# The v loads of all 24 tiles moved from SyncE's DMA queue to ScalarE's, with a priority for each kind of load and six buffers for a and v

## The chip, the cores and the metric

One core of one Trainium2 chip. The metric is the device time of one execution in microseconds, as the median of the runs of a kernel. Times are compared between kernels that ran in turn on the same chip.

## The reference, cut to what matters

```python
# B, H, S, D = 4, 8, 768, 40
def _attn_ref(r, k, v, w, a, b):
    state = zeros((B, H, D, D))
    for t in range(S):                                   # kt = k[:, :, t] and so on
        y[:, :, t] = einsum('bhd,bhde->bhe', rt, state)
        Sa = einsum('bhde,bhe->bhd', state, at)
        state = (state * wt[:, :, None, :] - einsum('bhd,bhe->bhde', Sa, bt)
                 + einsum('bhd,bhe->bhde', vt, kt))
    return y

def _moe_ref(x, w_theta, w_tok_r, w_tok_i, w_ch):        # x: y as [4, 768, 320]
    theta = x @ w_theta
    y = einsum('ts,bsd->btd', w_tok_r, x * cos(theta)) + einsum('ts,bsd->btd', w_tok_i, x * sin(theta))
    u = x + y
    return u + maximum(u @ w_ch, 0.0)
```

The kernel cuts each sequence of 768 steps into 6 chunks of 128. That makes 24 tiles of 128 steps by 8 heads by 40 features. Each tile needs one load of w, k, b, a and v, of 160 KB each, and half of a pair of r loads.

## The kernel before, the parts that matter

All work is a list of operations. A list scheduler in Python, run when the kernel is built, orders them from tuned priorities and a model of their costs; each engine then runs its operations strictly in that order.

```python
    raw_w = sb("raw_w", [128, H, D], FP32, 4)
    raw_a = sb("raw_a", [128, H, D], FP32, 4)
    raw_kb = sb("raw_kb", [128, 2, H, D], FP32, 4)
    raw_v = sb("raw_v", [128, H, D], FP32, 4)
    # ... load(i) gives for tile i the buffers i % 4 and the sources
    #     ap[bi, :, ci * C:(ci + 1) * C, :].rearrange("h t d -> t h d"), so pieces of 40 floats

    def evac(eng, kind, i, psk, dst, n, reads=(), writes=()):
        if eng == "ACT":
            add(eng, kind, i, lambda: copy_words(dst, ps(psk)[:, 0:n // 2]), 165 + n / 2.4, [psk], writes)
        # ... else the same on DVE

    def loads(i):
        for key, dst, src in load(i):                     # w, k, b, a, v
            add("SP", "load", i,
                lambda dst=dst, src=src: nc.sync.dma_start(out=dst, in_=src),
                650, [], [key], work=1030)
        # ... and two r loads for each pair of tiles, also on SyncE

    # ... prep, attention_scores, recurrence, readout, theta, mixing: all add() operations
    order = plan.order()
    table = "lnexp"
    for o in order:
        # ... a table load where ScalarE's function changes
        o.fn()
```

ScalarE (ACT) works between TensorE (PE) and its next inputs nearly everywhere. It copies transposed blocks and products out of PSUM, the memory that TensorE writes to (`evac`, `nx` and `nu`), and it makes the exponentials `ex`.

## Time and profile before

| | before |
|---|---|
| time, median of 3 runs | 215.06 us (214.36 to 215.53) |
| span in the profile | 212.6 us |
| TensorE busy | 195.1 us, 92% |
| ScalarE busy | 148.6 us, 70% |
| mean granted clock of TensorE | 1.00 |

The lines behind this stand in the prediction below.

### The profile page before, as it was taken

To read this page: it belongs to the slowest core of one execution; us is meant where nothing else is said; L and a number is where in the kernel's file an instruction comes from. 1 tells how busy PE (TensorE), PEld (TensorE's weight loads), DVE (VectorE), ACT (ScalarE), POOL (GpSimd) and SP (SyncE) were. 2 spreads that over 40 slices of the span, in tenths; PEclk is the share of its full clock that TensorE was granted. 3 is DMA by queue.
4 is the path that set the end of the run, shared out by engine and by line. 5 is a ranking of instruction groups with operands and counts; after the bars stand their busy time and mean duration, and the time that the engine had idled before them with its cause. 6 is when DMAs were issued, how large, how long until landed. Compare 5 with 4: busy or idle time off the path is not lost.

```text
span 212.6 us, 8107 instructions
## 1 busy us (share of the span) xinstructions
PE 195.1 (92%) x3344; PEld 156.3 (74%) x3344; DVE 165.5 (78%) x252; ACT 148.6 (70%) x340; POOL 117.4 (55%) x173
## 2 busy tenths in 40 slices
PE   1686899888998999999999999999999999999993
PEld 1464777776786777888878888887788887777771
DVE  7537796989889779869897889978979899744533
ACT  3375858799989969968787676599967996642101
POOL 5003358578765997857688315477667488050000
PEclk9999999999999999999999999999999999999999
DMA  7998989999799999975999899977997110011222
GB/s 118 221 191 170 178 166 175 177 181 185 148 162 194 162 166 193 190 123 111 244 161 197 163 180 178 183 133 172 183 201 145 35 34 3 0 34 71 84 96 93
DMA packets 134181, 30.82 MB, mean 145 GB/s; under 512 B 125824, under 2 KB 134144, under 8 KB 134144
## 3 DMA queue, kind: packets, MB, share of 16 engines
q1 hardware_dynamic: 131712, 27.54, 66.1%
q0 software_dynamic: 2432, 2.77, 8.8%
q8 instruction: 26, 0.43, 0.9%
q14 instruction: 11, 0.09, 0.1%
HBM read 29.13 MB, written 3.93 MB: 156 GB/s over the span
## 4 chain that ended last, share of the span: by engine, by line
PE 78%; DVE 7%; ACT 4%; issue 4%; DMA 3%; POOL 2%; SPq 1%; DVEq 0%; ACTq 0%; POOLq 0%
PE ps_s L724 19%; PE ps_s L398 13%; PE ps_d L522 11%; PE ps_s L670 9%; PE ps_s L625 4%; PE ps_s L573 3%; PE ps_s L505 3%; PE ps_s L591 2%; DVE phi L527 2%; PE ps_s L654 2%; DVE psi L527 2%; PE ps_s L772 2%; DMA raw_v<-in_v_dram 2%; PE ps_d L448 2%; PE ps_s L652 2%
## 5 line engine op out<-in xcount | busy, mean ns | idle before, releaser
L468 POOL TENSOR_TENSOR kb<-raw_kb,ex 128x320 bf16<-128x320 f32 x44 | 37.3, 863 | 32.4 <-ACT ex L460 30.9
L724 PE MATMUL ps_s<-zr,wtok_r 128*128 128x320 bf16 x144 | 40.7, 300 | 0.0
L724 PE MATMUL ps_s<-zi,wtok_i 128*128 128x320 bf16 x144 | 40.6, 299 | 0.0
L527 DVE TENSOR_TENSOR psi<-ps_d,mask_p 128x1024 bf16<-128x1024 f32 x24 | 29.3, 1220 | 7.4 <-PE ps_d L522 7.3
L527 DVE TENSOR_TENSOR lamu<-ps_d,mask_p 128x1024 bf16<-128x1024 f32 x24 | 29.3, 1220 | 4.7 <-PE ps_d L522 4.2
L527 DVE TENSOR_TENSOR lamv<-ps_d,mask_p 128x1024 bf16<-128x1024 f32 x24 | 29.1, 1218 | 3.0 <-PE ps_d L522 2.9
L527 DVE TENSOR_TENSOR phi<-ps_d,mask_n 128x1024 bf16<-128x1024 f32 x24 | 29.2, 1217 | 0.7 <-PE ps_d L522 0.6
L472 POOL TENSOR_TENSOR ah<-raw_a,ex 128x320 bf16<-128x320 f32 x22 | 19.0, 863 | 16.3 <-ACT ex L460 7.6
L706 POOL TENSOR_TENSOR zr<-cs,x 128x320 bf16<-128x320 f32 x23 | 17.8, 791 | 12.9 <-ACT cs L694 12.9
L460 ACT ACTIVATE ex<-ps_d 128x648 f32<-128x648 f32 x24 | 17.2, 716 | 7.7 <-PE ps_d L456 4.6
L734 DVE TENSOR_TENSOR u<-ps_s,x 128x320 bf16<-128x320 f32 x24 | 11.7, 489 | 11.2 <-PE ps_s L724 11.1
L401 ACT COPY uT<-ps_s 128x192 f32<-128x192 f32 x24 | 7.7, 320 | 17.1 <-PE ps_s L625 17.0
L706 POOL TENSOR_TENSOR zi<-cs,x 128x320 bf16<-128x320 f32 x23 | 17.7, 791 | 2.1 <-ACT cs L694 2.0
L522 PE MATMUL ps_d<-aT,kbT 64*128 64x128 bf16 x384 | 17.2, 222 | 1.1 <-ACT aT L401 0.5
L401 ACT COPY kbT<-ps_s 128x512 f32<-128x512 f32 x24 | 14.3, 595 | 4.6 <-PE ps_s L398 3.9
L724 PEld LDWEIGHTS <-wtok_r 128*128 128x128 bf16 x144 | 14.0, 97 | 4.5
L724 PEld LDWEIGHTS <-wtok_i 128*128 128x128 bf16 x144 | 14.0, 98 | 3.6
L398 PE MATMUL ps_s<-ident,kb 128*128 128x128 bf16 x192 | 15.4, 223 | 1.3 <-DVE kb L468 1.3
L743 DVE SCALAR_TENSOR_TENSOR oo<-ps_s,u 128x320 f32<-128x320 f32 x24 | 11.6, 486 | 5.2 <-PE ps_s L670 5.2
L522 PEld LDWEIGHTS <-kbT 64*128 64x128 bf16 x384 | 11.6, 96 | 5.2 <-issue 1.7
L654 PE MATMUL ps_s<-kb,lamu 128*128 128x40 bf16 x192 | 15.0, 180 | 0.5 <-DVE lamu L527 0.4
L652 PE MATMUL ps_s<-kb,lamv 128*128 128x40 bf16 x192 | 15.4, 180 | 0.0
(113 smaller groups left out, 556.3 us busy)
## 6 DMA issues: line engine op xcount, KB each, us to landing
raw_w<-in_w_dram SPq DMA_DIRECT2D x24, 160.0 KB, 3.8
raw_kb<-in_k_dram SPq DMA_DIRECT2D x24, 160.0 KB, 4.3
raw_kb<-in_b_dram SPq DMA_DIRECT2D x24, 160.0 KB, 4.2
raw_a<-in_a_dram SPq DMA_DIRECT2D x24, 160.0 KB, 4.1
raw_v<-in_v_dram SPq DMA_DIRECT2D x24, 160.0 KB, 3.9
raw_r<-in_r_dram SPq DMA_DIRECT2D x24, 160.0 KB, 3.5
out_dram<-oo SPq DMA_DIRECT2D x24, 160.0 KB, 2.3
wrow_r<-in_moe_w_tok_r_dram POOLq DMA_DIRECT2D x6, 192.0 KB, 4.7
```

The costliest lines, as they stand in the source:

```text
L398: nc.tensor.transpose(out=dst[:, c:c + 128], in_=pair(src, g), identity=ident)
L401: nc.scalar.copy(out=out.bitcast(FP32), in_=in_)
L460: add("ACT", "exp", i, lambda: nc.scalar.activation(out=ex, in_=ps(pk).rearrange("p a b -> p (a b)")[:, 512 - DM:512 + DM + 8], func=AF.Ex ...
L468: lambda j=j: (nc.vector if fast else nc.gpsimd).tensor_tensor(out=paired(kb[:, j])[:, :, :, 0:D], in0=natural(raw_kb[s4][:, j]), in1=invW ...
L472: lambda: (nc.vector if fast else nc.gpsimd).tensor_tensor(out=paired(ah)[:, :, :, 0:D], in0=natural(raw_a[s4]), in1=Wi, op=ALU.mult),
L522: nc.tensor.matmul(t[:, q, g, :], lhsT=lhs[rows(q), g * 128:(g + 1) * 128], rhs=rhs[rows(q), g * 128:(g + 1) * 128], start=True, stop=True)
L527: add("DVE", kindm, i, lambda: nc.vector.tensor_tensor(out=dst.rearrange("p a b c -> p (a b) c"), in0=ps(p).rearrange("p a (g c) -> p (a g ...
L652: nc.tensor.matmul(o, lhsT=lamv[:, p, g, :], rhs=kb[:, 0, h, 0:D], start=first, stop=False, skip_group_check=True)
L654: nc.tensor.matmul(o, lhsT=lamu[:, p, g, :], rhs=kb[:, 1, h, 0:D], start=False, stop=True, skip_group_check=True)
L670: nc.tensor.matmul(dst, lhsT=lhs[:, kt, :], rhs=rhs[:, kt, :], start=kt == 0, stop=kt == 2)
L706: nc.vector if fast else nc.gpsimd).tensor_tensor(
L724: nc.tensor.matmul(ps(pk)[:, 0:DM], lhsT=wtok[nm][:, s, j * 128:(j + 1) * 128], rhs=zs[c][:, s], start=n == 0 and c == 0, stop=n == NT - 1 ...
```

## The change

The intent: SyncE's queue is one line, in which a v load stands behind everything else. A second issuing engine lets v come when its own priority says, and deeper buffers for a and v allow earlier loads.

```diff
+SECOND = dict(v=24)
-SP_DEPTH = 3600.0
+SP_DEPTH = 4600.0
@@ priorities: now also one correction per operation, and a term for PE changing its mode
-            o.prio = 1000.0 * (TIMES[o.spec[0]][o.spec[1]] + OFF[o.spec[2]])
+            o.prio = 1000.0 * (TIMES[o.spec[0]][o.spec[1]] + OFF[o.spec[2]] + ADJ.get(o.idx, 0.0))
@@ buffers
-    raw_a = sb("raw_a", [128, H, D], FP32, 4)
+    raw_a = sb("raw_a", [128, H, D], FP32, 6)
-    raw_v = sb("raw_v", [128, H, D], FP32, 4)
+    raw_v = sb("raw_v", [128, H, D], FP32, 6)
@@ loads
+        last = None
         for key, dst, src in load(i):
-            add("SP", "load", i,
-                lambda dst=dst, src=src: nc.sync.dma_start(out=dst, in_=src),
-                650, [], [key], work=1030)
+            name = key[0][4:]
+            if i < SECOND.get(name, 0):
+                add("ACT", "l" + name, i,
+                    lambda dst=dst, src=src: nc.scalar.dma_start(out=dst, in_=src),
+                    430, [], [key], work=930, after=[last])
+            else:
+                last = add("SP", "l" + name, i,
+                    lambda dst=dst, src=src: nc.sync.dma_start(out=dst, in_=src),
+                    600, [], [key], work=930)
@@ cut: all numbers of OFF, TIMES, WAIT, TSWITCH tuned anew; ADJ, a table of 1,456 numbers
```

The scheduler's model charges ScalarE 430 ns for an issue.

## The prediction

> **What bounds the kernel now.** I read first the page's busy times, then the table of stretches (busy time of every engine, clock and DMA share by window), then the chain of work that ended last, the waits of the SyncE queue, and last the queue's timeline.
>
> ```profile
> span 212.6 us, 8107 instructions
> PE 195.1 (92%) x3344; PEld 156.3 (74%) x3344; DVE 165.5 (78%) x252; ACT 148.6 (70%) x340; POOL 117.4 (55%) x173
> ```
>
> TensorE is busiest, but 92% is an average over two very different halves. The table of stretches shows it (columns: window, its length, then busy us and instructions of PE, PEld, DVE, ACT, POOL, then clock, DMA share, GB/s):
>
> ```profile
> 0.00:20.00 20.00, 11.51 (x157) 8.84 (x157) 11.93 (x56) 10.60 (x22) 4.04 (x15) 1.00 0.97 174
> 20.00:70.00 50.00, 44.95 (x907) 36.26 (x908) 42.75 (x46) 41.56 (x98) 33.40 (x49) 1.00 0.97 175
> 70.00:100.00 30.00, 29.50 (x532) 24.16 (x530) 24.48 (x34) 24.27 (x54) 25.11 (x37) 1.00 0.91 160
> 100.00:160.00 60.00, 59.93 (x1097) 49.00 (x1095) 52.00 (x68) 46.96 (x108) 36.58 (x52) 1.00 0.93 180
> 160.00:212.60 52.60, 49.16 (x664) 38.01 (x661) 34.35 (x53) 25.16 (x62) 18.23 (x24) 1.00 0.20 58
> ```
>
> See two things. From 100 us on PE never idles (59.93 of 60), so nothing done there shortens the run unless it removes PE work. Until 70 us PE does idle while the DMA engines are 97% busy: that is the stage in which loads, and the order in which they are used, can matter.
>
> Busy PE is not productive PE, so I separate work from loss. The chain gives the pace of PE when nothing holds it:
>
> ```profile
> 97.50 0.51 PE ps_s L670 x3
> ...
> 113.18 0.45 PE ps_s L505 x8
> 113.62 0.55 PE ps_d L522 x16
> ...
> 202.73 3.53 PE ps_s L724 x26
> ```
>
> A 320-column matmul costs 3.53/26 = 136 ns, a 128-column transposition 0.45/8 = 56 ns; 16 of the score matmuls that use 64 rows (L522) take 0.55 us, about 29 ns each beside some 0.1 us when PE changes between 64 and 128 rows. 80- and 40-column matmuls run at 36 and 25 to 27 ns, by their distance in the timeline. With these paces for all 3344 matmuls PE has 172 us of work; its order holds 65 blocks of 64-row matmuls, so 130 changes at about 0.11 us (14.5 us). Sum 186.5. The first matmul starts at 4.1 and the last matmul's start lies 3.6 us before the end. So 212.6 - 186.5 - 4.1 - 3.6 = 18.4 us is loss. By start-to-start distances the loss is 8.8 us in 0 to 20, 7.3 in 20 to 70, 1.3 in 70 to 100, about 1 after it.
>
> I use one number per place: time minus PE work already done ("lag"). It is 4.1 at the start and can only rise; the end is total work + final lag + 3.6. In the kernel before it is 9.8 when the second tile's prefix-sum matmuls start, 14.9 at tile 4, 16.7 at tile 6, 18.7 at tile 8, 21.1 at tile 12, and 21.1 still at tile 23. A change helps by exactly what it takes off the final lag of 21.1.
>
> ```profile
> SPq L746 <- DVE oo L743: 48.2, 17, 12.4
> SPq L417 <- POOL kb L468: 11.2, 9, 2.7
> ```
>
> and in that queue's timeline (start, length):
>
> ```profile
> 91.59 0.54 SPq L417 DMA_DIRECT2D raw_kb<-in_b_dram  x1
> 95.82 0.36 SPq L746 DMA_DIRECT2D out_dram<-oo  x1
> ```
>
> The SyncE queue is one line: a load behind a store waits until the output is computed (here from 92.1 to 95.8), a k or b load behind a full buffer until GpSimd has read it. Landings of w by the trace: tile 6 at 37.6, tile 9 at 57.0, tile 14 at 93.0, tile 17 at 122.0; the last v lands at 163.8.
>
> **What the Trainium skill says.** "DMA: Bandwidth & Descriptors", section "Issuing engines are not separate DMA queues": DMAs of the scalar, sync and gpsimd engines run on the same 16 DMA engines, and a second issuer "will only save the time on the sequencer". The trace agrees that the engines, not the queue, are full: share 0.97 for 70 us. Same page, "Queues, rings and completion order": each DMA engine round-robins between the queues with work; so a v load on a second, nearly empty queue need not stand behind the SyncE backlog (landing now 3.9 us after issue, median), but delays that backlog by as much. No run shows this yet. Same page, "Why small descriptors are slow": a fixed cost per packet. The page's 125,824 packets under 512 B (rows of 40 floats, 160 B) fit: 66.1% of 212.6 us on 16 engines over 131,712 packets is 17 ns each. "ScalarE: Activation LUTs", section "What ACT_TABLE_LOAD costs": about 1283 ns; the trace has 1.28 us.
>
> **The change part by part.**
> 1. The 24 v loads leave SyncE for ScalarE. An unblocked issue takes 0.54 to 0.6 us in the queue's timeline; 24 x 0.57 = 13.7 us more on ACT's sequencer, 148.6 to 162 of some 210 us. Partly on the path: ACT feeds PE nearly everywhere (evacuations).
> 2. ACT's order has 10 table loads in place of 12: 2 x 1.28 = 2.6 us less ACT.
> 3. PE's instructions are the same in number and shape, in a new order with 67 blocks of 64-row matmuls: 4 more changes x 0.11 = +0.45 us of PE.
> 4. The order at the start: w, both r, a, k, b of tile 0, then w of tile 1; v comes only after ACT's copy of r. k and b of tile 0 move from second and third to fifth and sixth place: at 0.9 us a load about 3 us later. In exchange PE transposes r, and starts tile 1's prefix sums, before the first scores. Now the first x0 product (L561) starts at 10.2; I expect about 14, but with 3.1 rather than 2.0 us of work done. The second started at 21.5 (work 7.9); with tile 1 prepared it should start near 19.5 (work 8.3). Lag there: 13.6 before, about 11 after.
> 5. After the start, loads of w, a come earlier and a and v have six buffers, so fewer waits for buffers. DMA idle time until 100 us is 0.03 x 70 + 0.09 x 30 = 4.8 us; I let the change recover most of it, 4 us.
> 6. The order of use is tighter: PE meets tile 14's prefix sums after 68.3 us of its work (78.4 before), its k/b transpositions after 76.3 (81.7), tile 17's prefix sums after 98.5 (104.7).
>
> The sum. I take the place where the data come latest against the order. Tile 14's b: ahead of it in the new order lie about 61 strided SyncE loads, 13 or 14 v and 18 r loads, against 73 strided and 14 r before, but one or two fewer weight rows: 1.5 x 0.95 + 4 x 0.5 - 1.5 x 1.1 = about +1.8 us. It landed at 94.8, so 96.6 at the old pace, 92.6 with 4 us recovered, and GpSimd's product (863 ns) and the hop make 93.7. Lag 93.7 - 76.3 = 17.4. Tile 17's w: the same number of loads ahead as before; landed at 122.0, of which the stores' waits between 90 and 122 are some 5 us; 122 - 4 - 3 (I let half the stores' waits go) + 0.6 = 115.6, lag 17.1. So data allow a final lag of about 17.4; engine waits lay on top of the data's limit before (its highest data limit was 19.4, the actual 21.1), so I add 0.6: 18. Gain 21.1 - 18 = 3.1, less 0.45 for changes of mode: 2.65. That gives 215.06 - 2.65 = 212.4. The whole order was made anew with a correction for every operation, which speaks for losses among ACT, DVE and PE that I cannot read from counts; for that I take another 1.2 us off: **211.2 us**.
>
> **Rivals.**
> - *The DMA engines bind as before and no idle time is recovered.* For: share 0.97 until 70 us, same bytes, same packets. Then lag at tile 14 is 96.6 + 1.1 - 76.3 = 21.4 and the tighter order of use gains nothing: 215 to 216.
> - *The search found better filling of PE than I credit, and two queues keep the DMA engines full past 90 us.* Share was only 0.91 and 0.93 after 70 us. Lag 14 to 16: 208 to 210.
> - *ACT blocks in its own issues.* SyncE's issues take up to 2 us when the queue is full (1.99 at 84.02). If ACT's 24 take 1.5 us each, ACT gains 36 us and evacuations stall PE: 216 to 220. Against: ACT's queue has one or two transfers in flight, so it should not fill.
> - *Hidden anyway*: after 100 us PE is solid, so deeper buffers late give nothing; that is why I expect no gain there.
>
> **Range and chances.** The first rival has perhaps one chance in four, the second two in five, the third one in fifteen. Range for eight in ten: 206.5 to 215.5. More than 2% faster is below 210.8: 0.45; within 2%: 0.48; slower: 0.07.
>
> **What would show it.** Right: PE idle in 0 to 100 us falls from 14 us by a few us, most of it before 70; v loads on ACT's queue with issues near 0.6 us; PE solid after 100; last load landing before 160. Wrong: DMA share above 0.97 with PE waiting for kb or w of tiles 10 to 17 (first rival); long ACT issues and waits of PE for ACT (third); a lag that rises after 120 us, from work postponed to the end.

## More of the kernel before

One more view is needed later, the table of stretches with finer cuts. Its columns are the window and its length, then busy microseconds and (instructions) of PE, PEld, DVE, ACT and POOL, then the granted clock of TensorE, the DMA engines' share and GB/s. The share adds up the time of all packets over 16 engines and can pass 1. The kernel before:

```profile
40.00:50.00 10.00, 8.94 (x194) 7.43 (x194) 8.53 (x9) 9.39 (x21) 8.43 (x13) 1.00 0.93 172
```

ScalarE is busy 9.39 us of the 10 between 40 and 50 us. At that place it has little slack for anything that makes it stand still.

## The result, and the profile after

| | before | after |
|---|---|---|
| time, median | 215.3 us (4 runs, 214.36 to 215.91) | 222.37 us (4 runs, 221.90 to 224.01) |
| ratio | | 1.0346 (95% interval 1.0277 to 1.0415) |
| span in the profile | 212.6 us | 221.0 us |
| mean granted clock of TensorE | 1.00 (profile) | 0.981 to 0.991 (all runs) |

A ratio here is the mean time of one kernel's fast runs over that of the other's of the same rounds, so it is not quite the ratio of the medians. The change made the kernel 3.5% slower. The prediction of 211.2 us was wrong, and so was its range.

The page of the changed kernel, the lines that answer to those shown of before (in the last line a digit is the granted clock in a fortieth of the span, in tenths, 9 being 90% or more):

```profile
span 221.0 us, 8049 instructions
PE 198.1 (90%) x3344; PEld 160.2 (72%) x3344; DVE 165.7 (75%) x252; ACT 147.8 (67%) x338; POOL 117.7 (53%) x173
...
PEclk9999999679999999999999999999999999999999
```

TensorE has the same 3344 instructions but 3.0 us more busy time, and a dip of its clock near 40 us that before does not have. The table of stretches of the changed kernel says where the time went:

```profile
0.00:20.00 20.00, 9.28 (x105) 7.34 (x105) 10.44 (x53) 9.08 (x17) 4.11 (x15) 1.00 1.04 174
20.00:70.00 50.00, 44.65 (x837) 36.93 (x832) 38.33 (x41) 35.20 (x89) 28.55 (x40) 0.93 1.06 184
70.00:100.00 30.00, 26.64 (x523) 22.05 (x523) 24.18 (x31) 24.28 (x54) 23.36 (x34) 1.00 0.77 139
100.00:160.00 60.00, 59.99 (x1044) 49.27 (x1042) 49.40 (x66) 47.42 (x107) 41.15 (x59) 1.00 1.00 183
```

Against before, TensorE is busy 2.2 us less in the first 20 us. In 20 to 70 us it runs 837 matmuls where before ran 907, and in 70 to 100 us it is busy 2.9 us less. After 100 us it is full in both. With the prediction's method (distances from start to start, less each matmul's own pace) the loss grows from 8.8 to 11.1 us in 0 to 20, from 6.0 to 9.0 in 20 to 60 and from 1.7 to 5.5 in 60 to 80. That is 9.1 us more; after 80 us before lost some 1 us and the changed kernel nothing, and the span grew by 8.4. So all of the loss comes before 80 us. The DMA engines did not move less there: between 20 and 70 us it was 184 GB/s, against 175 before. Nor did v land sooner after its issue on the second queue: the page gives 4.4 us (median) against 3.9 before, and w took 4.6 against 3.8.

ScalarE's timeline shows the event (start, length, engine, line, what; in brackets how long it stood idle before, and what released it). The changed kernel near 40 us:

```profile
37.62 0.71 ACT L670 ACTIVATE ex<-ps_d 128x648 f32<-128x648 f32 x1
40.46 0.44 ACTq L623 DMA_DIRECT2D raw_v<-in_v_dram  x1
41.00 0.44 ACT L787 ACTIVATE nu<-ps_s 128x320 bf16<-128x320 f32 x1 [2.68 <-DMA raw_kb<-in_k_dram]
```

The evacuation `nu` is said to have waited for a load of k, which it does not read. The only thing between is the issue of a v load. The chain of waits of the same kernel has the same order:

```profile
36.40 4.04 DMA raw_kb<-in_k_dram
40.44 0.02 issue
40.46 0.44 ACTq L623
...
41.00 0.45 ACT nu L787
41.45 0.04 issue
41.49 0.62 PE ps_s L801 x7
```

A load of k, issued by SyncE, lands at 40.44. At that moment, and no earlier, ScalarE issues its v load, and TensorE gets `nu` at 41.49. In TensorE's timeline this is a hole:

```profile
38.86 0.20 PE L801 MATMUL ps_s<-v,kb 128*128 128x80 bf16 x1
41.49 0.23 PE L801 MATMUL ps_s<-nu,kb 128*128 128x80 bf16 x1 [2.44 <-ACT nu L787]
```

After the hole comes the dip of the clock. The changed kernel by stretches of 2 us, the clock being the third number from the end:

```profile
40.00:42.00 2.00, 0.51 (x9) 0.51 (x9) 0.31 (x1) 1.00 (x3) 2.00 (x5) 0.57 1.08 204
42.00:44.00 2.00, 2.00 (x42) 1.80 (x39) 1.05 (x3) 0.65 (x2) 1.25 (x2) 0.50 1.34 225
44.00:46.00 2.00, 2.00 (x23) 1.80 (x20) 2.00 (x2) 0.66 (x3) 0.00 (x0) 0.50 1.32 182
46.00:48.00 2.00, 2.00 (x25) 1.70 (x23) 0.28 (x1) 1.59 (x5) 0.00 (x0) 0.72 0.91 161
48.00:50.00 2.00, 1.76 (x45) 1.43 (x43) 1.32 (x2) 1.46 (x3) 1.23 (x3) 1.00 1.01 167
```

TensorE counts as fully busy from 42 to 46 us, at half speed: a busy PE that does half its work. The trace's own record of the clock has only two values here, 1 and 0.50, and it holds 0.50 for 6.83 us, from 40.28 us on; 0.57 and 0.72 are means of a stretch. Not every hole is followed by this: after the holes of 3.29 us at 4.65 and of 2.63 us at 12.27 in the same kernel no lower clock is recorded.

### The theory, and its rivals

The instruction list of the compiled kernel shows why a v load waits for a k load. Loads and stores of SyncE and ScalarE together count on eight completion semaphores (DMAHW0 to DMAHW7), handed out in turn along the program. Each later load waits, before it is issued, until the transfer that had its semaphore last, the one eight places earlier, has landed. From that list, SyncE's loads around the first v load, and v loads on ScalarE (cut):

```
SyncE    8 raw_kb_75<-in_b_dram  [waits DMAHW0_49]
SyncE    9 raw_kb_75<-in_k_dram  [waits DMAHW1_49]
SyncE   10 raw_w_66<-in_w_dram   [waits DMAHW2_49]
SyncE   11 raw_r_85<-in_r_dram   [waits DMAHW4_49]
ScalarE  5 raw_v_78<-in_v_dram   [waits DMAHW3_49]      tile 0
ScalarE 11 raw_v_79<-in_v_dram   [waits DMAHW1_49]      tile 1
ScalarE 58 raw_v_83<-in_v_dram   [waits DMAHW0_49]      tile 5
```

SyncE skips number 3, because the v load of tile 0 took it. The list comes from building the kernel. Its trace bears it out: the 168 transfers of the two queues count on eight semaphore numbers, 21 each, and each v load in the table below has the number of its partner. Counting eight places back in the program order of both queues gives a partner for each v load. The six v loads that ScalarE was seen waiting at, against the landings in the trace of the changed kernel:

| v load of tile | eight places before it | landed at | v issued at | ScalarE idle before the issue |
|---|---|---|---|---|
| 0 | a of tile 0 | 7.29 | 7.31 | 1.30 us |
| 1 | k of tile 1 | 13.62 | 13.65 | 2.29 us |
| 4 | k of tile 5 | 34.45 | 34.47 | 0.90 us |
| 5 | k of tile 6 | 40.44 | 40.46 | 2.14 us |
| 10 | w of tile 13 | 70.88 | 70.90 | 1.29 us |
| 11 | b of tile 12 | 77.16 | 77.18 | 1.53 us |

All six follow their partner's landing by 0.02 us (some of the rounded numbers differ by 0.03). None of these v loads has any other business with its partner, and each issue itself is short (0.37 to 0.45 us). "Perfetto Trace Analysis", section "DMA Instruction — HWDGE (DVE, Sync)" in the Trainium skill puts this wait on the sequencer, ahead of the reported start of the instruction. The trace agrees: the issue at 40.46 is 0.44 us long, and its wait shows only as idle time of the evacuation behind it.

- **Theory A.** ScalarE, which runs in order, stands at its v issues until an unrelated SyncE load lands, 9.4 us in all. The evacuations behind stand with it, TensorE idles, and where it idles long its clock is halved.
- **Theory B.** The retuned order and priorities are worse in themselves, whoever issues.
- **Theory C.** A second queue, or each issue on ScalarE, costs time of its own.

### The profile page after: what moved, and what is told of

The parts are those of the page before. It is cut to its first block, busy times and chain, and to the rows that moved or that the text cites. A ratio compares the mean times of both kernels' runs of the same rounds, so it can differ in the third digit from the quotient of the medians.

```text
span 221.0 us, 8049 instructions
## 1 busy us (share of the span) xinstructions
PE 198.1 (90%) x3344; PEld 160.2 (72%) x3344; DVE 165.7 (75%) x252; ACT 147.8 (67%) x338; POOL 117.7 (53%) x173
## 4 chain that ended last, share of the span: by engine, by line
PE 76%; DMA 10%; SPq 6%; ACT 3%; issue 1%; DVE 1%; ACTq 1%; POOL 1%; POOLq 0%
PE ps_s L934 18%; PE ps_s L601 13%; PE ps_d L732 11%; PE ps_s L880 9%; DMA raw_kb<-in_k_dram 5%; SPq L627 4%; PE ps_s L835 4%; DMA raw_kb<-in_b_dram 3%; PE ps_s L801 3%; SPq L636 2%; PE ps_s L783 2%; PE ps_s L864 2%; PE ps_s L715 2%; DMA raw_v<-in_v_dram 2%; PE ps_s L862 2%; PE ps_s L982 2%
## 5 line engine op out<-in xcount | busy, mean ns | idle before, releaser
L732 PE MATMUL ps_d<-aT,kbT 64*128 64x128 bf16 x384 | 18.9, 229 | 2.9 <-ACT ex L670 2.6
L732 PEld LDWEIGHTS <-kbT 64*128 64x128 bf16 x384 | 12.1, 99 | 6.6 <-issue 4.0
L787 ACT ACTIVATE nu<-ps_s 128x320 bf16<-128x320 f32 x24 | 10.7, 444 | 8.6 <-PE ps_s L783 5.8
L601 PE MATMUL ps_s<-ident,kb 128*128 128x128 bf16 x192 | 16.1, 231 | 0.1
L880 PE MATMUL ps_s<-wth,xT 128*128 128x320 bf16 x72 | 14.0, 304 | 1.4 <-ACT nuT L604 1.3
```

Source lines behind the costliest of these rows:

```text
L601: nc.tensor.transpose(out=dst[:, c:c + 128], in_=pair(src, g), identity=ident)
L732: nc.tensor.matmul(t[:, q, g, :], lhsT=lhs[rows(q), g * 128:(g + 1) * 128], rhs=rhs[rows(q), g * 128:(g + 1) * 128], start=True, stop=True)
L880: nc.tensor.matmul(dst, lhsT=lhs[:, kt, :], rhs=rhs[:, kt, :], start=kt == 0, stop=kt == 2)
```

## The experiments

Seventeen kernels ran. All results are correct but for the four marked as wrong. Runs of the kernel before: 215.5 to 215.9 us.

### 1. All v loads back on SyncE

```diff
-                    lambda dst=dst, src=src: nc.scalar.dma_start(out=dst, in_=src),
+                    lambda dst=dst, src=src: nc.sync.dma_start(out=dst, in_=src),
```

> The changed kernel with every v load issued by SyncE at the same place of the emitted order; six buffers, priorities and the order of all other instructions stay. Theory A (the issues of v on ScalarE stand waiting for the landing of an older load and hold up the evacuations behind them, six waits of 0.9 to 2.3 us, 9.4 us in all, before 80 us): no ScalarE wait of that kind is left, the clock dip at 40 to 47 us is gone, and the kernel takes 210 to 216 us, 6 to 11 us less than the changed kernel's 222. Theory B (the retuned order and priorities are themselves worse, whichever engine issues): 220 to 224 us, and the idle time of TensorE before 80 us stays near 25 us. Theory C (two queues slow the DMA engines or delay SyncE's loads): as A in time, but the DMA share and the time per load would change while ScalarE's waits were harmless.

Measured: 216.62 us (216.01 to 217.46), ratio to before 1.0044 (1.0000 to 1.0089). That is 5.75 us less than the changed kernel (6.5 us by the ratios), with its order otherwise untouched. It lies 0.6 us above Theory A's range. The clock is 1.00 again. This run with v on SyncE, by stretches:

```profile
0.00:20.00 20.00, 11.50 (x137) 8.65 (x137) 11.91 (x56) 10.87 (x22) 5.81 (x17) 1.00 0.95 174
20.00:70.00 50.00, 43.85 (x880) 35.49 (x881) 41.22 (x44) 37.76 (x92) 30.49 (x43) 1.00 0.96 172
70.00:100.00 30.00, 29.72 (x566) 24.85 (x564) 25.30 (x33) 25.05 (x60) 25.93 (x37) 1.00 1.01 184
```

137 matmuls in the first 20 us against 105, and 880 against 837 in the next 50. Theory B falls as the main cause. Theory C is not settled here, since the loads do land sooner with one queue (w 4.3 us after its issue against 4.6, v 4.0 against 4.4); experiments 5 and 8 settle it. But this order is not faster than the old one either, which is a second question.

### 2. Only the six that waited, and only the other eighteen

```diff
+WAITED = (0, 1, 4, 5, 10, 11)
-                    lambda dst=dst, src=src: nc.scalar.dma_start(out=dst, in_=src),
+                    lambda dst=dst, src=src, q=nc.sync if i in WAITED else nc.scalar: q.dma_start(
+                        out=dst, in_=src),        # six_scalar: the two engines exchanged
```

> The changed kernel with only the six v loads whose issue was seen waiting (tiles 0, 1, 4, 5, 10, 11) moved to SyncE; the other 18 stay on ScalarE. Theory A: nearly the whole loss comes back with a quarter of the issues moved, 211 to 217 us, within 2 us of the run that moves all 24. A theory in which each issue on ScalarE costs its own 0.4 us, or in which the second queue slows the DMA engines: three quarters of the loss stays, about 219 to 221 us.

> The reverse: only the v loads of tiles 0, 1, 4, 5, 10 and 11 issued by ScalarE, 18 by SyncE. Theory A: most of the loss stays, 218 to 223 us, with waits of ScalarE on older loads before 80 us. Theory of a cost for each issue or of the second queue: a quarter of the loss, about 214 to 216 us.

Measured: 220.55 us (ratio 1.0225) with the six on SyncE, and 225.25 us (1.0434) with only the six on ScalarE. The first expectation missed: most of the loss stayed. The second got its waits, 11.2 us of them, but was slower than its range and than the changed kernel itself. The trace of the first shows why it missed. ScalarE's timeline of the kernel with the six on SyncE:

```profile
40.09 0.77 ACT L672 ACTIVATE ex<-ps_d 128x648 f32<-128x648 f32 x1
44.48 0.37 ACTq L624 DMA_DIRECT2D raw_v<-in_v_dram  x1
44.95 0.42 ACT L779 CAST nx<-ps_s 128x320 bf16<-128x320 f32 x1 [4.09 <-DMA raw_w<-in_w_dram]
```

The v load of tile 6, which did not wait in the changed kernel, now waits 3.6 us. Moving six issues changed who comes eight places before whom: its partner is now w of tile 7, which lands at 44.46. Two more waits came (0.6 and 1.1 us, ended by a and b of tile 9 landing at 54.61 and 57.13, their listed partners), and the clock fell again, to a mean of 0.974. So the run doesn't test a quarter of the issues against three quarters, as it was meant to. It does show that the wait is a matter of a v load's place among the others, not of the tile. Six issues that wait 11.2 us cost more than 24 that wait 9.4, which no cost per issue can give.

### 3. The kernel before, with nothing but v moved to ScalarE

```diff
-                lambda dst=dst, src=src: nc.sync.dma_start(out=dst, in_=src),
+                lambda dst=dst, src=src, q=nc.scalar if key[0] == "raw_v" else nc.sync: q.dma_start(
+                    out=dst, in_=src),
```

> The kernel before, with nothing changed but that ScalarE issues its v loads at the places where SyncE did (four buffers, old order and priorities). Theory A: ScalarE now waits both for the v buffer to come free and for an older load's landing, because the old order puts loads as early as SyncE can stand waiting: far slower, 225 to 260 us. Theory B (order alone at fault): about 215 us plus at most 2 us for 24 issues of 0.4 us.

Measured: 223.51 us, ratio 1.0352 (1.0309 to 1.0395), so the old order loses as much as the new one. It is below Theory A's range, but far above the 217 us that the issues alone would give. One wait stands out, 4.5 us, and it is again ended by a load eight places before (b of tile 8). By the start-to-start account 7.0 of the 8.7 us that this kernel loses beyond the kernel before lie in 40 to 60 us, around that wait. The timeline of ScalarE in that run:

```profile
42.92 0.48 ACT L442 ACTIVATE lw<-raw_w 128x320 bf16<-128x320 f32 x1
47.89 0.37 ACTq L417 DMA_DIRECT2D raw_v<-in_v_dram  x1
48.31 0.44 ACT L578 ACTIVATE nu<-ps_s 128x320 bf16<-128x320 f32 x1 [4.90 <-DMA raw_kb<-in_b_dram]
```

### 4. Stops of ScalarE without any load on its queue

v on SyncE as in experiment 1, and idle copies on ScalarE at the six places:

```diff
+    def v_load(i, dst, src):
+        nc.sync.dma_start(out=dst, in_=src)
+        for _ in range(DELAY.get(i, 0)):
+            nc.scalar.copy(out=idle_out, in_=idle_in)        # 128x512, read by nobody
+DELAY = {0: 3, 1: 5, 4: 2, 5: 5, 10: 3, 11: 3}   # delays_six; delay_one: {5: 5}; delays_cal: {0: 2, 1: 4, 4: 1, 5: 3, 10: 2, 11: 2}
```

> The run with all v loads on SyncE (216.6 us), with ScalarE given idle work in place of the six waits: after the places of the v loads of tiles 0, 1, 4, 5, 10, 11, 3, 5, 2, 5, 3 and 3 copies of 128x512 into a tile nobody reads, 0.45 us each, so 1.35, 2.25, 0.9, 2.25, 1.35 and 1.35 us, 9.5 us in all against the 9.4 us seen waiting. No load is on ScalarE's queue. Theory A (what costs is ScalarE standing still at these places, not the queue): 220 to 224 us, the changed kernel's time. A theory in which the second queue itself or its contention costs: 216 to 218 us.

> The same with only one stop, the 2.25 us at the v load of tile 5, near 40 us. If one stop costs no more than its length: at most 218.9 us (216.6 + 2.25), and less where ScalarE has slack. If TensorE's clock is halved for about 5 us after a stop of more than 2 us: a clock of 0.5 in a stretch after 40 us in the record, and up to 219 to 221 us.

Measured: 221.32 us (1.0278) with six stops and 216.99 us (1.0061) with one. But the copies were longer than I had thought. The timeline of ScalarE with one stop:

```profile
34.51 3.21 ACT L625 COPY idle_out<-idle_in 128x512 f32<-128x512 f32 x5
```

That is 0.64 us a copy, so the six stops came to 13.5 us, not 9.5. The dose was too large, and I ran it again:

> The six stops again with the right length. The copies of the earlier two runs took 0.64 us each in the trace, not 0.45, so that the stops there came to 13.5 us in place of 9.4. Now 2, 4, 1, 3, 2 and 2 copies, 1.3, 2.6, 0.6, 1.9, 1.3 and 1.3 us, 9.0 us in all. If ScalarE's standing still is the whole cause: 219 to 222.5 us. If it is half of it and the second queue the other half: 217 to 219 us.

Measured: 221.24 us (219.99 to 222.01), ratio 1.0259 (1.0208 to 1.0310). With 9.0 us of stops and no load on ScalarE's queue at all, 4.6 of the 5.75 us are there (of 6.5 us by the ratios). Between this and the changed kernel (1.0346, interval 1.0277 to 1.0415) the intervals overlap, so these runs don't show a rest that needs another cause.

But the sum agrees better than the places do. By the start-to-start account the profiled run lost 2.6 us more than the run of experiment 1 before 80 us, where the changed kernel lost 7.5 us more, and 2.2 us more in 100 to 160 us, where the changed kernel lost nothing. In that stretch TensorE is busy 59.25 us with v on SyncE, and with these stops:

```profile
100.00:160.00 60.00, 57.49 (x996) 46.27 (x994) 47.72 (x64) 44.37 (x98) 38.46 (x55) 1.00 0.95 179
```

Part of that late loss is TensorE waiting for v and k or b to be made ready, with v loads of SyncE landing at 143.8 and 156.0 us. The larger dose of 13.5 us lost 5.6 us more before 80 us. So stops of ScalarE alone do cost time, but this run does not show that stops of the measured length make the same loss at the same places.

The one stop is the other half of the lesson. It was followed by a hole of 2.76 us in TensorE's work and by half clock, as in the changed kernel. By stretches, the kernel with one stop:

```profile
36.00:38.00 2.00, 0.00 (x0) 0.00 (x0) 0.75 (x1) 1.94 (x5) 1.68 (x3) 1.00 1.09 255
38.00:40.00 2.00, 1.90 (x39) 1.70 (x40) 0.98 (x2) 1.17 (x4) 1.57 (x3) 0.63 1.16 196
40.00:42.00 2.00, 2.00 (x28) 1.80 (x24) 1.74 (x2) 0.41 (x3) 0.40 (x1) 0.52 1.06 192
42.00:44.00 2.00, 2.00 (x36) 1.71 (x35) 0.61 (x1) 2.00 (x6) 0.00 (x0) 1.00 1.29 200
```

So a hole that was made in another way was followed by the same dip (0.50 for 3.41 us in the clock's record). Yet the stop cost only 0.4 us of time. Experiment 7 returns to that.

### 5. v on GpSimdE's queue, and the order planned anew

```diff
-                    lambda dst=dst, src=src: nc.scalar.dma_start(out=dst, in_=src),
+                    lambda dst=dst, src=src: nc.gpsimd.dma_start(out=dst, in_=src),      # v_pool
```
```diff
-SECOND = dict(v=24)
+SECOND = dict(v=0)      # replanned, in another kernel: the scheduler itself now sees v on SyncE
```

> The changed kernel with the v loads issued by GpSimdE, whose DMAs count on semaphores of their own (eight others). Theory A: ScalarE never stands waiting for a load, so 212 to 219 us; GpSimdE pays about 0.6 us for each issue (14 us on an engine that is 53% busy), part of which may delay k, b and a. If any second queue beside SyncE's does the damage: 220 us or more.

> The changed kernel with the plan told that SyncE issues every load (priorities, constants and six buffers kept): the order of all engines is planned anew. Theory A: no wait of ScalarE on loads, 212 to 218 us, near the run with v moved to SyncE. If the gain were in the retuned order for a second queue and this order is spoilt by replanning: above 218 us.

Measured: v on GpSimdE 216.02 us (1.0026). A second queue is harmless when its issuer counts on other semaphores and is not ScalarE. That holds although GpSimdE paid 0.93 us for an issue and not 0.6, and although the loads landed no sooner than in the changed kernel (w 4.6 us and v 4.8 us after their issue, against 4.6 and 4.4). So slower landings on two queues, the rest of Theory C, are not what costs. The replanned kernel took 229.29 us (1.0634), a clear miss. A new start-to-start account gives it 32.8 us of TensorE loss against 20.7 in experiment 1, spread over the first 80 us and again later, up to 208 us. The priorities, one for every operation, were tuned for one sequence of decisions; that another sequence spoils them is likely, and no run shows it. It tells nothing about the queue.

### 6. Is it buffers, or the order of the loads?

```diff
-    raw_a = sb("raw_a", [128, H, D], FP32, 4)      # and raw_v: before_six
+    raw_a = sb("raw_a", [128, H, D], FP32, 6)
```
```diff
-    order = plan.order()
+    order = by_need(plan.order())   # loads sorted by their first reader, each as early as its buffer allows
```

> The kernel before with six buffers for a and for v and nothing else changed. The trace of before shows SyncE's queue held by the DMA engines (share 0.9 to 1.0 up to 100 us) rather than by buffers, so both theories expect the same time, 214 to 216.5 us; less would say that buffers were a limit.

> An attempt at a version that beats both: the kernel before with six buffers for a and v, all loads on SyncE, and the loads re-sorted by the place of their first reader in the emitted order, each as early as its buffer allows. If the supply of loads in the order of need sets the lag of TensorE (21.1 us in before, where an order strictly by need, at 0.95 us a load, would allow about 18): 212 to 215 us. If the lag comes from elsewhere, 215 to 217 us.

> The changed kernel's order of the engines with all loads on SyncE, re-sorted by need in the same way. Worked out from the order of its first readers at 0.95 us a load, the loads allow a lag of about 21.7 us, against the 22.8 us of the run with v on SyncE: 214.5 to 216.5 us. That would say that the retuned order asks for its loads earlier than the old one (21.7 against 17.8 us) and can't win while the DMA engines are full.

Measured: six buffers alone 215.81 us (1.0031, interval 0.997 to 1.0092): nothing, as expected. The sorted loads failed twice: 224.07 us (1.0390; one of the four runs was slow) on the old order and 231.20 us (1.0737) on the new one. On the old order TensorE's loss agrees with the six-buffer kernel's within 0.1 us in each 10 us from 20 to 110 us, so the sorting changed nothing there. Then a store stands behind a row of loads, and TensorE behind the store. Two lines of the waits of that kernel between 60 and 135 us (total, times, longest):

```profile
DVE oo L775 <- DMA out_dram<-oo: 6.7, 1, 6.7
...
PE ps_s L702 <- DVE oo L775: 5.9, 1, 5.9
```

On the new order TensorE stands idle for 11.1 us from 116.2 us, while DVE's `oo` waits 11.3 us for a store.

I found no version that beats both kernels.

### 7. Short loads: what the supply of data is worth

The same bytes and instructions, but each load of w, k, b, a and v reads a contiguous stretch: 1,280 bytes a row in place of pieces of 160. The results are wrong on purpose.

```diff
-            return ap[bi, :, ci * C:(ci + 1) * C, :].rearrange("h t d -> t h d")
+            flat = ap[bi].rearrange("h s d -> (h s d)")
+            return flat[ci * C * DM:(ci + 1) * C * DM].rearrange("(t h d) -> t h d", t=C, h=H)
```

> The kernel before with every w, k, b, a and v load reading one contiguous 160 KB stretch of the same input, 1,280 bytes a row, in place of 1,024 pieces of 160 bytes: same bytes, same instructions, wrong results on purpose. The r loads, which read such rows already, take about 0.5 us of the DMA engines against 0.95. If the supply of loads bounds the first 80 us: faster than 215.5 by 4 us or more, 203 to 211 us. If not: 213 to 216 us.

> The changed kernel with the same contiguous loads, v still issued by ScalarE. This takes the wait away and leaves the issue: older loads have landed when ScalarE comes to its next v. Theory A (waits for older loads): the six waits are gone or below 0.5 us, and the time is within 2 us of the next run, which has the same loads all on SyncE. A cost of the second queue or of each issue of its own: 3 to 6 us above the next run, as with the real loads.

> The same with all v loads on SyncE. With before_wide it tells what the retuned order is worth where loads are no limit: if it is better in itself, 2 us or more below before_wide; if it is no better, the same or above. Range 203 to 213 us.

Measured:

| | real loads | short loads |
|---|---|---|
| before | 215.5 to 215.9 us | 214.39 us (ratio 0.9937) |
| new order, v on SyncE | 216.62 us (1.0044) | 212.75 us (0.9852) |
| new order, v on ScalarE | 222.37 us (1.0346) | 224.84 us (1.0401) |

The row of the kernel before is the surprise. Its stretch of 20 to 70 us with short loads, to be held against 44.95 of 50 us busy at a DMA share of 0.97 with real ones:

```profile
20.00:70.00 50.00, 45.22 (x913) 36.54 (x913) 42.59 (x46) 42.13 (x99) 33.40 (x49) 1.00 0.73 197
```

The DMA engines have a quarter of their time free and TensorE idles as before. So the full DMA engines did not bound the old order. Its own sequence of dependences between the engines remains, or its four buffers (six were tried with the real loads only); no run shows which. In the new order, v on SyncE, the same stretch with short loads:

```profile
20.00:70.00 50.00, 47.06 (x964) 38.95 (x964) 44.72 (x49) 41.33 (x100) 33.98 (x50) 1.00 0.73 204
```

964 matmuls in place of 880. The new order is better than the old by 0.8% where loads are short (1.6 us; the expectation asked for 2). With real loads the two come out even, which fits an order that asks for its loads earlier and so meets the limit of supply that the old one didn't.

With v on ScalarE the waits did not vanish but grew to 15.8 us, so that expectation failed. ScalarE's timeline of that kernel:

```profile
4.93 0.72 ACT L708 CAST r<-raw_r 128x640 bf16<-128x640 f32 x1
12.22 0.38 ACTq L624 DMA_DIRECT2D raw_v<-in_v_dram  x1
12.63 0.37 ACT L605 COPY aT<-ps_s 128x256 f32<-128x256 f32 x1 [6.98 <-DMA raw_r<-in_r_dram]
```

The build put the loads of both queues in another common order here. The load eight places before the first v load is now the first r load of the second pair, for tiles 2 and 3 (before, a of tile 0), and it lands when v is issued. The wait was meant to go away and instead got a new partner. That is Theory A again, by accident.

### 8. Issues on ScalarE where none was seen waiting, and the one stop with short loads

```diff
+                    lambda dst=dst, src=src, q=nc.scalar if i >= 12 else nc.sync: q.dma_start(      # late_scalar
```

> The changed kernel with v of tiles 0 to 11 on SyncE and of tiles 12 to 23 on ScalarE, where the changed kernel's trace shows no wait at any of these issues. Theory A: without waits an issue on ScalarE is all but free (0.4 us on an engine with slack), so 216 to 217.5 us, the time with all on SyncE (216.6). If the second queue or the issues cost something themselves: half of what the six stops leave unexplained and more, 218 us or above.

> The one stop of 3.2 us at the v load of tile 5, now with the contiguous loads (wrong results on purpose), where loads are no limit and the run without a stop takes 212.75 us. With real loads the stop cost 0.4 us though TensorE stood idle for 2.9 us and its clock was halved for some 4 us. If the supply of loads hid it there: 3 to 5 us here, 215.5 to 218 us, with the clock at 0.5 for a stretch after the stop. If ScalarE's slack hid it: under 1 us here too.

Measured with the later twelve on ScalarE: 220.16 us, ratio 1.0158 (1.0103 to 1.0213). The expectation failed, and its trace settles the question that it was run for. (The run with the profile counts as slow, being 1.75% above the fastest; the fast runs are 218.23, 220.03 and 220.30 us. So this trace is read for the place of the loss and not for its size.) The first of the twelve issues waits, ScalarE's timeline:

```profile
83.23 0.72 ACT L671 ACTIVATE ex<-ps_d 128x648 f32<-128x648 f32 x1
87.48 0.47 ACTq L623 DMA_DIRECT2D raw_v<-in_v_dram  x1
87.99 0.43 ACT L891 COPY th<-ps_s 128x320 f32<-128x320 f32 x1 [4.04 <-DMA raw_kb<-in_b_dram]
```

Eight places before it stands b of tile 13, which lands at 87.46. The hole and half the clock follow, and after that nothing more, with eleven more issues on ScalarE. The same kernel by stretches:

```profile
86.00:88.00 2.00, 0.00 (x0) 0.00 (x0) 0.00 (x0) 0.01 (x1) 1.47 (x2) 0.75 0.62 103
88.00:90.00 2.00, 1.53 (x9) 1.05 (x9) 0.00 (x0) 1.89 (x4) 0.89 (x2) 0.50 0.98 190
90.00:92.00 2.00, 2.00 (x27) 1.61 (x26) 0.80 (x1) 0.78 (x2) 0.78 (x1) 0.50 1.16 217
...
100.00:160.00 60.00, 59.96 (x1062) 49.30 (x1060) 49.34 (x66) 46.88 (x105) 40.79 (x59) 1.00 1.01 182
```

TensorE's loss is 6.0 us in 80 to 100 us (0.3 with all v on SyncE) and 0.6 us in 100 to 160 us (1.6 there). Eleven issues that don't wait cost nothing that can be seen, second queue and all. One that waits makes the whole difference. Theory C falls.

Measured with one stop and short loads: 215.15 us (0.9955), against 0.9852 without the stop, so it costs 2.4 us. That is below the 3 to 5 us expected but well above the 0.4 us with real loads. Each of the two differences is uncertain by about 1 us. With real loads TensorE would have idled a little later anyway: by the start-to-start account the stop added 3.1 us in 30 to 40 us, and 2.4 us less was lost in 40 to 50 us. With short loads it added 3.9 us and hardly any of it came back there (0.3 us). The price of a stop depends on what else is late at that moment. This fits that 9.4 us of waits cost 5.75 us in the changed kernel and 5.4 us of waits 7.7 us in experiment 3.

## Why the prediction was wrong, by its own steps

- **The step that failed: part 1, the cost of a v load on ScalarE, and with it the odds of the rival "ACT blocks in its own issues", put at one chance in fifteen.** Part 1 counted the issues and no wait ahead of them. The rival had the right direction, too small a size (216 to 220; it became 222.4) and another cause. What it was argued against with, "ACT's queue has one or two transfers in flight, so it should not fill", asked the wrong question. The issues stayed short (0.40 us on average, not 1.5). What stopped ScalarE was the wait ahead of the issue for a load of the other queue, which the list of instructions and their waits would have shown before any run. Six waits made 9.4 us, and without them the time was 5.75 us less (experiment 1). Of the prediction's own signs, TensorE's idle time in 0 to 100 us rose from 14.0 to 19.4 us in place of falling.
- **Part 1, 13.7 us of issues, "partly on the path".** It measured 24 x 0.40 = 9.6 us, and issues without a wait cost nothing that can be seen (experiment 8). The term of the sum that was missing is the wait.
- **Part 2 and part 3** can't be seen in the time. The table loads did fall from 12 to 10. The 67 blocks cost 0.5 us more in changes of mode by the same account (15.0 against 14.5), but that account takes over the 0.11 us for a change, so it is no test.
- **Part 4.** First x0 product: 14 predicted, 16.8 measured, 14.8 with v on SyncE. Second: 19.5 predicted, 24.6 measured, 21.6 with v on SyncE. The 3 us between the last two come with the waits of tiles 0 and 1; the other 2 us I had underrated.
- **Part 5, 4 us recovered from idle DMA engines.** Wrong in kind for the old order: with the DMA engines free a quarter of the time it gained 0.6% (experiment 7). So the place where the data came latest was not what set its end.
- **Part 6, a tighter order of use.** Right, and worth more than I let it be: with v on SyncE short loads take 1.9% off the new order, where they take 0.6% off the old. That is the first rival (215 to 216, "the tighter order of use gains nothing"), and it is what experiment 1 gives once the waits are out of the way: 216.6 us.
- **The last 1.2 us, for an order made anew.** A gain of this size shows only where loads are short: 212.75 against 214.39 us.
- **What was not in it:** half a clock after a hole. "TensorE: Matmul & The Clock Gate", section "What's actually happening", in the Trainium skill says so: the clock is 4/8 or 8/8 of full, and falls after an idle window of some 3.4 us. The trace agrees on the 0.50, for 6.83 us; its hole was shorter, 2.44 us.
- **Two slips in its readings.** SyncE's issues before took up to 3.94 us (at 67.31), not 2. And 186.5 + 21.1 + 3.6 makes 211.2 us, 1.4 us short of the span of 212.6, so the "final lag" of 21.1 is not quite the final one. Neither slip touches the wait.

What stays open: whether a rest of 1 to 2 us beside the waits is real (221.24 against 222.37 us, overlapping intervals), why the stops of experiment 4 lost part of their time after 100 us, and how much of the 5.75 us is the halved clock and how much the idle time. No run was made to part the two. In 60 to 80 us, where the clock stayed whole, the changed kernel still lost 5.5 us against 3.2 with v on SyncE.

## What to carry to other kernels

Before a load moves to an engine that also computes, look in the list of instructions for what its issue waits on, not only at how long it takes: a wait in an engine's own order stops everything behind it, even when it is for a transfer that has nothing to do with it. SyncE, which computes nothing, could mostly afford to stand waiting here (not when a store stood behind a row of loads, experiment 6). An engine that feeds the bottleneck can't. And a full resource isn't the bound until a run with that resource relieved gets faster: here relieving a DMA share of 0.97 made the old kernel only 0.6% faster.

## What the Trainium skill lacked or had wrong

- "DMA: Bandwidth & Descriptors", section "Issuing engines are not separate DMA queues", counts as the gain of a second issuer the sequencer time of issuing, "usually small relative to the DMA itself", and names no cost to the second issuer. Here the issue took 0.37 to 0.45 us, but the wait ahead of it, for the transfer that had used the same completion semaphore, took up to 2.3 us in the changed kernel and 3.5 to 6.6 us in others, and stopped the engine's compute for as long.
- "Perfetto Trace Analysis", section "DMA Instruction — HWDGE (DVE, Sync)", places the wait rightly, on the sequencer and outside the reported interval. It doesn't say how to find it when the issuer also computes: as idle time of the next compute instruction, released by a transfer which that instruction doesn't read (2.68 us before `nu` at 41.00).
- "TensorE: Matmul & The Clock Gate", section "What's actually happening", speaks of an idle window of about 3.4 us. Here shorter holes were followed by a clock of 0.50: one of 2.44 us for 6.83 us, one of 2.76 us for 3.41 us, and with the six stops of 9.0 us one of 1.36 us (at 62.9) for 3.41 us. Holes of 3.29 and 2.63 us in the first 15 us of the changed kernel were followed by none. So the length of a hole alone did not tell whether the clock would fall.
- No page that I read says that the price of a stop depends on what else is late: the same 3.2 us stop of ScalarE cost 0.4 us with real loads and 2.4 us with short ones (each uncertain by about 1 us).
